# A fused attention and two-MLP kernel: one group's v rows in another queue, and fixed places for some work of TensorE, ScalarE and VectorE

## The chip, the cores and the metric

One core of one Trainium2 chip. The metric is device time in microseconds for one execution, as the median of the runs; lower is better. The engines are TensorE (PE; its weight loads are PEld), VectorE (DVE), ScalarE (ACT), GpSimd (POOL) and SyncE (SP). Each runs its own queue of instructions in order; SP issues most of the DMAs.

## The reference, cut to what matters

```python
# attention: q, k, v are (2, 8, 768, 64), float32
k_sum = k.reshape(B, H, 24, 32, D).max(axis=3)
v_sum = v.reshape(B, H, 24, 32, D).mean(axis=3)
scores_l = where(|i - j| < 16, scale * q @ k.T, -1e9)        # local window
scores_s = scale * q @ k_sum.T + log(32)                     # 24 block summaries
a = softmax(concat([scores_l, scores_s]))                    # over both parts
x = a @ concat([v, v_sum])                                   # 1536 tokens x 512
# first MLP: 512 -> 2048 -> 512
h = maximum(x @ w_in, 0);  y = (h * h) @ w_out
# second MLP: 512 -> 1536 -> 512
xn = y / sqrt(mean(y * y) + 1e-6) * rms_g
out = (silu(xn @ w_gate) * (xn @ w_val)) @ w_out2
```

The MLP weights arrive as float64 and are turned into float32 on the chip.

## The kernel before, in words

Attention runs in 12 groups of 128 tokens, six to a batch. A group g goes through `scores(g)` (TensorE: a mask product, 32 small matmuls, and a second mask product for the first four groups), `softmax(g)` (DVE finds the maximum, ACT takes the exponentials head by head with their sum, DVE divides), `ptrans(g)` (TensorE transposes the probabilities, ACT copies them to pT) and `av(g)` (TensorE multiplies pT by the v rows in `vx`; the output of group 0 is called x0, of group 1 x1). `split_xs` then writes x as a high part (`xhi`, ACT) and a low part (`xlo`, DVE), because every MLP product is made of three float32r products. `qprep(g)` transposes q for groups g and g+1. `vx` has four slots; groups 0 and 1 fill them first.

The weights come in units of 512 KB: `load64` issues the DMA, `conv_a` (two ACT operations, L203 and L204) and `conv_b` (four DVE operations, L210 to L217) turn the words into float32, `split` (one ACT, one DVE operation, L223 and L224) makes the high and low parts. The first eight units are wi0 to wi3 and wo0 to wo3. The table `FIRST` (L227) says behind which other instruction conv_a (key 1) or conv_b (key 2) of a unit must come in its engine's queue.

The program is traced in one order, and a planner lays out each engine's queue from that order and from modelled times; it runs before the kernel is compiled. `after(...)` and `tc.issue_after` bind an instruction to come later than another in the queue of that same engine; they add no wait between engines. Buffers, PSUM banks and DMA landings add real waits.

At the seam between the two MLPs, `turn` transposes the normalised rows and forms their differences (`ta`, `xt`, `bt`). The second MLP multiplies half its columns by a scheme of seven products, for which `late(m)` (L899) makes the high and low parts of the operands T3 and T4 and `latest(m)` (L949) those of B22. `hsplit` (L619) makes the high and low parts (`hhi`, `hlo`) of a hidden tile, which the last `y` matmuls of the first MLP read.

Other names in the rows: `kr`, `qr`, `vr`, `raw_wi`, `raw_wo` are landed inputs, `pps`, `qps`, `xps`, `s`, `h`, `y` are PSUM tiles, `mx` and `sm` the maxima and sums of a softmax, `r` the squared hidden tile, `vsum` a sum of v for batch 1.

Of the kernel before, what the change touches and what calls it, by code (L numbers as in the profile page):

```python
# [10 lines left out]
F32 = mybir.dt.float32  # L11
# [4 lines left out]
ALU = mybir.AluOpType  # L16
# [16 lines left out]
def tile_window_attention_moe_moe2(  # L33
# [13 lines left out]
    nc = tc.nc  # L47
    B, H, S, D = q.shape
    NT, DM = out.shape
    P = 128  # L50
# [5 lines left out]
    NPAIR = H // 2  # L56
    QT = 64
    KW = QT + 2 * WIN
    NK = NB + KW
# [160 lines left out]
    def split(x, nm):  # L220
# [4 lines left out]
        return hi, lo  # L225

    FIRST = {  # L227
        (2, 0): [("mx", 0)], (2, 2): [("xlo", 0, 1)], (2, 3): [("xlo", 1, 1)],
        (1, 1): [("exp", 1)], (1, 2): [("xhi", 0, 1)], (1, 3): [("xhi", 1, 1)],
    }  # L230

    def combine(g, v_, f):
# [98 lines left out]
    def after(*marks):  # L331
        es = ExitStack()
        for m in marks:
            es.enter_context(tc.issue_after(mark[m].ins))
        return es
# [85 lines left out]
    def qload(g):  # L421
        b, r = divmod(g, GPB)
        state[("q", g)] = token_chunk(q, b, r // 2, f"qr{g}")

    def qprep(g):
        qr = state.pop(("q", g))
        qT2 = ap_.tile([P, NPAIR, 2 * P], F32, tag="qT", name=f"qT{g}", bufs=QB)
        for j in range(2):
            ps = psA(f"qps{g}_{j}", [P, NPAIR, P])
            for p in range(NPAIR):  # L430
                nc.tensor.transpose(ps[:, p, :], qr[:, j, p * P : (p + 1) * P], ident)
            with after(*((("exp", 1),) if g == 2 else ())):
                nc.scalar.mul(qT2[:, :, j * P : (j + 1) * P], ps, scale)
        state[("qT", g)] = state[("qT", g + 1)] = qT2

    def vmean(b, c):
# [41 lines left out]
    def scores(g):  # L478
        b, r = divmod(g, GPB)
        qT = state[("qT", g)][:, :, (r % 2) * P : (r % 2 + 1) * P]  # L480
        sl = [psA(f"s{e}_{g}", [P, NPAIR, NK]) for e in range(2)]
        wide = [P, NPAIR, NK]
        if g < NPE:
            for s_ in sl:
                mh = mhi["mid" if r else "first"]
                nc.tensor.matmul(s_, identr, mh.unsqueeze(1).to_broadcast(wide), start=True, stop=False)
        for p in range(NPAIR):
            for x in range(2):
                for e in range(2):
                    u = (e + x) % 2  # L490
                    o = STEP * (2 * r + u)
                    rr = slice(QT * e, QT * e + QT)
                    mark[("s", g)] = nc.tensor.matmul(  # L493
                        sl[e][QT * u : QT * u + QT, p, :],
                        qT[rr, p, QT * u : QT * u + QT],
                        kT[rr, p, o : o + NK],
                        start=g >= NPE, stop=g >= NPE,
                    )
        if g < NPE:
            for s_ in sl:  # L500
                mark[("s", g)] = nc.tensor.matmul(
                    s_, identr, mlo.unsqueeze(1).to_broadcast(wide), start=False, stop=True
                )
        state[("s", g)] = sl
# [66 lines left out]
    def av(g):  # L571
        pT = state.pop(("pT", g))
        ps = psA(f"xps1_{g}")
        for u in range(2):
            for p in range(NPAIR):
                o = p * P + QT * u
                for e in range(2):
                    nc.tensor.matmul(  # L578
                        ps[QT * e : QT * e + QT, o : o + QT],
                        vx[:, (2 * g + u) % NVX, 2 * p + e, :],  # L580
                        pT[:, e * NPAIR + p, QT * u : QT * u + QT],
                        start=True, stop=True,
                    )
        split_xs(ps, g, 1)
        state["done"] = g

# [13 lines left out]
    def hi_lo(hi, lo, s, n):  # L600
        sv = s[:, 0 : n * P].rearrange("d (k s) -> d k s", k=n)
        nc.scalar.copy(hi, sv)
        nc.vector.tensor_tensor(lo, sv, hi.bitcast(F32), op=ALU.subtract)


    def mm3(ps, pairs):
        tot = 3 * len(pairs)
# [10 lines left out]

    def hsplit(s, n, nm):  # L619
        hi, lo = t2(f"hhi{nm}", F32R), t2(f"hlo{nm}", F32R)  # L620
        nc.scalar.copy(hi[:, 0:n], s[:, 0:n])  # L621
        nc.vector.tensor_tensor(lo[:, 0:n], s[:, 0:n], hi[:, 0:n].bitcast(F32), op=ALU.subtract)  # L622
        return hi, lo

    def ff_out(ys, hh, ww, first, last):
# [106 lines left out]
        vm_load(0, c)  # L732
    vload(0)
    qload(2)
    for j in (0, LK - WIN):
        nc.gpsimd.memset(kT[:, :, j : j + WIN], 0.0)
    nc.gpsimd.memset(vx[0:WIN, 0], 0.0)
# [4 lines left out]
    qprep(0)  # L742
    prep_kend(0, nc.vector, 0, 4)
    prep_kend(0, nc.gpsimd, 4, NW1)
    with after("kend"):
        vload(1, nc.gpsimd)
    scores(0)
    softmax(0)
    scores(1)
# [11 lines left out]
    av(0)  # L761
    group(2)
    vload(2)
    rot["tags"] = ("y",)
    group(3)
    rot["tags"] = ("a", "x")
    av(1)
    vload(3)
    ptrans(2)
    qprep(4)  # L770
# [128 lines left out]
    def late(m):  # L899
        if m == 0:  # L900
            new_xs(2, "t")
        hi, lo = (t[:, :, m * P : (m + 1) * P] for t in xs[("t", 2)])
        hi_lo(hi, lo, rows.pop(m), KD)

    for i in range(n1 + 2):
        if i < n1:
            r, c, f = steps1[i]
            if c == 0:
                units1.until(("wi", f))
            if r == len(ROUNDS1) - 1 and c == NCH - 1:  # L910
                units1.cap = NW - 2
            ps = psB.tile([P, CH], F32, tag="h", name=f"h{c}_{f}", bufs=2)
            product(ps, W[("wi", f)], xs[(1, c)], 0, MT)
            t = square(ps, f"{c}_{f}")
            units1.tick()
            hq[i] = hsplit(t, CH, f"{c}_{f}")
        if i >= 2:
            r, c, f = steps1[i - 2]
            first = f == FIRST1[r]
            last = f == FIRST1[r] + ROUNDS1[r] - 1  # L920
            if c == 0:
                units1.until(("wo", f))
            if first:
                for m in range(MT):
                    ys[m] = y_tile(c, m, "y")
            ff_out([ys[m] for m in range(MT)], hq.pop(i - 2), W[("wo", f)], first, last)
            if c == NCH - 1:
                units1.used += 2
            if last:
                for m in range(MT):  # L930
                    gather(MT * c + m, ys.pop(m), r, ROUNDS1, "y", done1)
        if turns:
            turn()
        if i < n1 and norms:
            norm(norms.pop(0))
        if i == n1:
            for m in range(MT):
                late(m)


    hand.close()
# [68 lines left out]
    def pair(r, fill):  # L1010
        fs = (FIRST2[r], FIRST2[r] + 1)
        wg, wv, cs = {}, {}, {}
        for f in fs:
            units1.until(("wv", f))
            for d, kd in ((wg, "wg"), (wv, "wv")):
                d[f] = [
                    [half(t.rearrange("p (k f) -> p k f", k=KD), j) for t in W[(kd, f)]] for j in range(2)
                ]
            cm = W[("cm", f)]
            cs[f] = [[cm[:, e, j].rearrange("p (k f) -> p k f", k=K2) for e in range(2)] for j in range(4)]  # L1020
        A, C, z0, z1, v1 = {}, {}, {}, {}, {}
        for f in fs:
            A[f] = bank("h", f"qa{f}")
            six(A[f], wg[f][0], b1[0], True)
            z0[f] = t2(f"s{f}")
            nc.scalar.copy(z0[f], A[f])
        for f in fs:
            C[f] = bank("a", f"qb{f}")
            six(C[f], wg[f][1], b1[1], True)
            nc.vector.tensor_tensor(z0[f], C[f], z0[f], op=ALU.add)  # L1030
            nc.scalar.activation(z0[f], z0[f], AF.Silu)
        if r == 0:
            for m in (0, 2):
                latest(m)
        units1.tick()
        fill(fs[0])
        for f in fs:
            six(A[f], cs[f][1], x2_, False)
            z1[f] = t2(f"u{f}")
            nc.scalar.copy(z1[f], A[f])  # L1040
        for f in fs:
            C[f] = bank("a", f"qc{f}")
            six(C[f], cs[f][0], x1, True)
        units1.tick()
        for f in fs:
            six(A[f], cs[f][2], x3, False)
            v1[f] = t2(f"v{f}")
            nc.scalar.copy(v1[f], A[f])  # L1048
            nc.vector.tensor_tensor(v1[f], C[f], v1[f], op=ALU.add)  # L1049
        fill(fs[1])  # L1050
        units1.tick()
        for f in fs:
            six(A[f], wv[f][1], x4, False)
            nc.vector.tensor_tensor(z0[f], A[f], z0[f], op=ALU.mult)
            hq[(0, f)] = hsplit(z0[f], CH, f"z0_{f}")
        for f in fs:
            six(C[f], cs[f][3], b22, False)
            nc.vector.tensor_tensor(z1[f], C[f], z1[f], op=ALU.add)
            nc.scalar.activation(z1[f], z1[f], AF.Silu)
            nc.vector.tensor_tensor(z1[f], z1[f], v1[f], op=ALU.mult)  # L1060
            hq[(1, f)] = hsplit(z1[f], CH, f"z1_{f}")
        units1.tick()
# [86 lines left out]
```

## Time and profile before

| | us |
|---|---|
| median of 3 runs (lowest, highest) | 643.59 (642.15, 643.83) |
| the profiled execution | 642.17 |
| its span, first to last instruction | 640.5 |
| TensorE busy in the span | 622.3 (97%) |
| VectorE busy | 457.2 (71%) |
| ScalarE busy | 366.1 (57%) |
| mean granted TensorE clock, share of full | 0.994 |

The profiled execution is the fastest but one of the four known; 1.67 us of its time lie outside the span. Busy TensorE does not mean TensorE at its best: its clock has a lower level, and a matmul counts as busy for twice as long there.

### The profile page before, as it was taken

Reading aid. Unit: us, or ns where it says so; the run is one execution under the profiler, and the core shown is the slowest. Engines: PE = TensorE matmul, PEld = TensorE weight load, DVE = VectorE, ACT = ScalarE, POOL = GpSimd, SP = SyncE. Lnnn points to the kernel's source line nnn. Section 1 sums busy time; section 2 is a strip of 40 time slices with the busy share of each in tenths; the row PEclk is TensorE's granted clock in tenths of the full one; section 3 lists DMA queues with packets and bytes.
Section 4 is the critical chain, followed back from the end, with each engine's and each line's share of the span. In section 5 each row is a group of like instructions: output and inputs, shape, how many; then the busy total and the mean of one; then the engine's idle time right before and its main releaser. Section 6 shows DMA issues by size and latency. Waiting matters only on the chain.

```text
span 640.5 us, 9547 instructions
## 1 busy us (share of the span) xinstructions
PE 622.3 (97%) x3578; PEld 514.2 (80%) x3578; DVE 457.2 (71%) x830; ACT 366.1 (57%) x767; POOL 58.2 (9%) x87
## 2 busy tenths in 40 slices
PE   8879999999999999999999999999999999999997
PEld 6467887888888888888888788888888888888885
DVE  3789767969995299985487779489499499561323
ACT  5677676677673267564554667457357277353241
POOL 5012210000000000000000000003004004012040
PEclk9979999999999999999999999999999999999999
DMA  9999812446232123311020105218528429017063
GB/s 252 294 208 196 160 40 50 120 144 192 71 106 92 34 65 100 99 67 34 0 92 8 34 36 195 67 35 180 116 66 161 103 65 183 15 13 120 1 99 98
DMA packets 84430, 64.19 MB, mean 100 GB/s; under 512 B 50368, under 2 KB 73920, under 8 KB 84384
## 3 DMA queue, kind: packets, MB, share of 16 engines
q1 hardware_dynamic: 72976, 51.32, 27.1%
q0 software_dynamic: 11408, 12.26, 13.5%
q8 instruction: 28, 0.46, 0.3%
q14 instruction: 18, 0.15, 0.1%
HBM read 49.94 MB, written 13.63 MB: 99 GB/s over the span
## 4 chain that ended last, share of the span: by engine, by line
PE 86%; DVE 5%; SPq 4%; DMA 2%; ACT 2%; issue 1%; ACTq 0%
PE h L611 19%; PE y L631 18%; PE z L631 15%; PE qa L965 10%; PE v L611 5%; PE g L611 5%; PE qc L965 5%; PE qb L965 3%; SPq L358 2%; PE xps L578 1%; PE s L493 1%; PE pps L555 1%; SPq L474 1%; DMA raw_wi<-in_moe_w_in_dram 1%; PE xps L595 1%
## 5 line engine op out<-in xcount | busy, mean ns | idle before, releaser
L611 PE MATMUL h<-xhi,w_wi 128*128 128x512 f32 (+1 forms) x480 | 132.1, 349 | 0.0
L631 PE MATMUL y<-w_wo,hhi 128*128 128x512 f32 x384 | 117.0, 393 | 2.1 <-ACT hhi L621 1.6
L611 PEld LDWEIGHTS h<-xhi,w_wi 128*128 128x128 f32 x480 | 84.7, 189 | 12.0 <-ACT t L535 0.2
L631 PE MATMUL z<-w_wp,hhiz 128*128 128x512 f32 x288 | 85.7, 390 | 0.0
L631 PEld LDWEIGHTS y<-w_wo,hhi 128*128 128x128 f32 x384 | 71.3, 188 | 17.7 <-ACT hhi L621 2.3
L611 PE MATMUL h<-xlo,w_wi 128*128 128x512 f32 (+1 forms) x240 | 83.4, 349 | 0.4 <-DVE xlo L569 0.3
L1000 POOL DMA_DIRECT2D out_dram<-zs x40 | 35.0, 1131 | 498.9 <-ACT zs L996 496.5
L631 PE MATMUL y<-w_wo,hlo 128*128 128x512 f32 x192 | 72.4, 392 | 0.0
L631 PEld LDWEIGHTS z<-w_wp,hhiz 128*128 128x128 f32 x288 | 53.9, 188 | 11.1
L631 PE MATMUL z<-w_wp,hloz 128*128 128x512 f32 x144 | 53.0, 389 | 0.0
L790 ACT ACTIVATE r<-h 128x512 f32<-128x512 f32 x48 | 28.7, 597 | 38.7 <-PE h L611 38.7
L611 PEld LDWEIGHTS h<-xlo,w_wi 128*128 128x128 f32 x240 | 45.4, 189 | 6.5 <-DVE xlo L569 1.0
L791 DVE TENSOR_TENSOR r<-h,r 128x512 f32<-128x512 f32 x48 | 32.9, 685 | 21.5 <-ACT r L790 21.3
L631 PEld LDWEIGHTS y<-w_wo,hlo 128*128 128x128 f32 x192 | 35.7, 188 | 7.4 <-issue 0.2
L621 ACT CAST hhi<-r 128x512 fp32r<-128x512 f32 x48 | 29.7, 620 | 18.4 <-DVE r L791 18.1
L622 DVE TENSOR_TENSOR hlo<-r,hhi 128x512 fp32r<-128x512 f32 x48 | 32.8, 684 | 7.4 <-ACT hhi L621 7.1
L611 PE MATMUL g<-x,w_wg 128*128 128x512 f32 x144 | 34.6, 389 | 0.0
L611 PE MATMUL v<-x,w_wv 128*128 128x512 f32 x144 | 34.6, 389 | 0.0
L996 ACT COPY zs<-z 128x512 f32<-128x512 f32 x48 | 26.8, 591 | 11.9 <-PE z L631 11.0
L1049 DVE TENSOR_TENSOR v<-qc,v 128x512 f32<-128x512 f32 x12 | 8.3, 692 | 34.3 <-ACT v L1048 34.3
L631 PEld LDWEIGHTS z<-w_wp,hloz 128*128 128x128 f32 x144 | 27.0, 188 | 5.7
L611 PEld LDWEIGHTS g<-x,w_wg 128*128 128x128 f32 x144 | 27.0, 188 | 5.6
(206 smaller groups left out, 1222.9 us busy)
## 6 DMA issues: line engine op xcount, KB each, us to landing
out_dram<-zs POOLq DMA_DIRECT2D x40, 256.0 KB, 6.4
raw_wi<-in_moe_w_in_dram SPq DMA_DIRECT2D x16, 512.0 KB, 5.2
raw_wo<-in_moe_w_out_dram SPq DMA_DIRECT2D x16, 512.0 KB, 4.8
raw_wg<-in_moe_w_gate_dram SPq DMA_DIRECT2D x12, 512.0 KB, 3.5
raw_wv<-in_moe_w_val_dram SPq DMA_DIRECT2D x12, 512.0 KB, 3.6
raw_wp<-in_moe_w_out_dram SPq DMA_DIRECT2D x12, 512.0 KB, 5.5
kr<-in_k_dram SPq DMA_DIRECT2D x12, 256.0 KB, 4.1
qr<-in_q_dram SPq DMA_DIRECT2D x12, 256.0 KB, 5.1
```

The costliest lines, as they stand in the source:

```text
L358: nc.sync.dma_start(t[:, j].rearrange("p (h d) -> p h d", h=H), src[b, :, o : o + P, :].rearrange("h p d -> p h d"),)
L474: (eng or nc.sync).dma_start(vx[j : j + n, i0 + u], v[b, :, o : o + n, :].rearrange("h s d -> s h d"))
L611: pe["last"] = nc.tensor.matmul(ps, a_, b_, start=(i == 0), stop=(i == tot - 1))
L621: nc.scalar.copy(hi[:, 0:n], s[:, 0:n])
L622: nc.vector.tensor_tensor(lo[:, 0:n], s[:, 0:n], hi[:, 0:n].bitcast(F32), op=ALU.subtract)
L631: pe["last"] = nc.tensor.matmul(y, a_[:, ms], b_, start=(first and i == 0), stop=(last and i == 2))
L790: nc.scalar.activation(t, ps, AF.Relu)
L791: nc.vector.tensor_tensor(t, ps, t, op=ALU.mult)
L965: last = nc.tensor.matmul(ps, w[a_][:, kk], x[b_][:, kk], start=start and n == 0, stop=n == 3 * K2 - 1, skip_group_check=not start,)
L996: nc.scalar.copy(s, ys.pop(m))
L1000: nc.gpsimd.dma_start(out[g * P : (g + 1) * P, :], s, accum_op=ALU.add)
L1049: nc.vector.tensor_tensor(v1[f], C[f], v1[f], op=ALU.add)
```

## The change

The four DMAs of group 1's v rows leave POOL's queue, where they followed the last k summary copy, for SP's queue, where they follow the load of the second weight, wi1; that load is now written right behind `qload(2)`. In TensorE's queue every matmul of av(1) comes behind the scores of group 2, and every small matmul of scores(3) behind av(1); av(1) is written before group 3. Four entries of `FIRST` change: conv_a of wi1 comes behind the q copy for group 2 and the pT copy of group 1, conv_b of wi2 behind the maxima of group 2, conv_a of wi3 behind the exponentials of group 2. The casts and subtractions of `late` and `latest` come behind the last `hsplit` in the queues of ACT and DVE.

```diff
     FIRST = {
-        (2, 0): [("mx", 0)], (2, 2): [("xlo", 0, 1)], (2, 3): [("xlo", 1, 1)],
-        (1, 1): [("exp", 1)], (1, 2): [("xhi", 0, 1)], (1, 3): [("xhi", 1, 1)],
+        (2, 0): [("mx", 0)], (2, 2): [("mx", 2)], (2, 3): [("xlo", 1, 1)],
+        (1, 1): [("qT", 2), ("pT", 1)], (1, 2): [("xhi", 0, 1)], (1, 3): [("exp", 2)],
     }
...
-                nc.scalar.mul(qT2[:, :, j * P : (j + 1) * P], ps, scale)
+                mark[("qT", g)] = nc.scalar.mul(qT2[:, :, j * P : (j + 1) * P], ps, scale)
...
+                    with after(*((("av", 1),) if g == 3 else ())):
+                        mark[("s", g)] = nc.tensor.matmul(   # scores, arguments as before
...
+                    with after(*((("s", 2),) if g == 1 else ())):
+                        mark[("av", g)] = nc.tensor.matmul(  # av, arguments as before
...
+    def behind_h():
+        es = ExitStack()
+        for i in pe["h"]:
+            es.enter_context(tc.issue_after(i.ins))
+        return es
...
     def hsplit(s, n, nm):
         hi, lo = t2(f"hhi{nm}", F32R), t2(f"hlo{nm}", F32R)
-        nc.scalar.copy(hi[:, 0:n], s[:, 0:n])
-        nc.vector.tensor_tensor(lo[:, 0:n], s[:, 0:n], hi[:, 0:n].bitcast(F32), op=ALU.subtract)
+        pe["h"] = (
+            nc.scalar.copy(hi[:, 0:n], s[:, 0:n]),
+            nc.vector.tensor_tensor(lo[:, 0:n], s[:, 0:n], hi[:, 0:n].bitcast(F32), op=ALU.subtract),
+        )
...
     qload(2)
+    units1.load(2)
+    vload(1)
...
-    with after("kend"):
-        vload(1, nc.gpsimd)
...
     group(2)
     vload(2)
+    av(1)
     rot["tags"] = ("y",)
     group(3)
     rot["tags"] = ("a", "x")
-    av(1)
...
             for m in range(MT):
-                late(m)
+                with behind_h():
+                    late(m)
...
             for m in (0, 2):
-                latest(m)
+                with behind_h():
+                    latest(m)
```

## Rows read from the trace of the kernel before

**Rows 1.** The page, granted TensorE clock in tenths, 40 slices of 16 us.

```profile
PEclk9979999999999999999999999999999999999999
```

**Rows 2.** Waits of TensorE: who, for whom, total us, times, longest us.

```profile
PE pps L555 <- DVE t L545: 4.4, 2, 4.2
...
PE y L631 <- ACT hhi L621: 1.6, 2, 1.2
```

**Rows 3.** Windows: length, busy PE, PEld, DVE, ACT, POOL, clock, DMA share, GB/s.

```profile
24.70:64.00 39.30, 31.34 (x373) 25.83 (x373) 32.33 (x64) 29.39 (x86) 7.74 (x6) 0.91 1.08 235
34.00:36.00 2.00, 0.00 (x0) 0.00 (x0) 2.00 (x7) 2.00 (x13) 0.00 (x0) 0.74 1.04 236
36.00:42.00 6.00, 4.81 (x45) 4.06 (x46) 3.99 (x9) 5.22 (x23) 1.44 (x2) 0.52 0.98 156
```

**Rows 4.** Timeline of PE: start, us, instructions, idle before and its releaser.

```profile
26.04 0.57 PE L578 MATMUL xps<-pT,vx 120*64 120x64 f32 x12
29.08 0.70 PE L486 MATMUL s<-mstage 128*128 128x480 f32 x2 [2.48 <-ACT pT L558]
...
32.31 0.70 PE L501 MATMUL s<-mstage 128*128 128x480 f32 x2
37.19 1.08 PE L555 MATMUL pps<-ident,t 128*120 128x128 f32 x4 [4.18 <-DVE t L545]
38.06 1.06 PE L431 MATMUL qps<-ident,qr 128*128 128x128 f32 x4
```

**Rows 5.** Timeline of ACT, early stretch.

```profile
26.84 0.66 ACT L203 ACTIVATE x_wi<-raw_wi 128x512 f32<-128x512 f32 x1 [2.53 <-DMA raw_wi<-in_moe_w_in_dram]
...
33.54 0.36 ACT L535 ACTIVATE t<-s,mx 128x120 f32<-128x120 f32 x1 [1.27 <-DVE mx L529]
```

**Rows 6.** Timeline of DVE, early stretch.

```profile
27.54 0.43 DVE L210 TENSOR_SCALAR x_wi<-x_wi 128x512 f32<-128x512 f32 x1 [2.85 <-ACT x_wi L203]
...
30.67 0.69 DVE L224 TENSOR_TENSOR w_wi<-x_wi,w_wi 128x512 fp32r<-128x512 f32 x1 [0.68 <-ACT w_wi L223]
...
32.79 0.65 DVE L529 TENSOR_REDUCE mx<-s 128x4 f32<-128x480 f32 x1
...
39.69 0.17 DVE L543 TENSOR_SCALAR sm<-sm 128x8 f32<-128x8 f32 x1 [1.20 <-ACT t L535]
...
42.78 0.69 DVE L569 TENSOR_TENSOR xlo<-xps,xhi 128x512 fp32r<-128x512 f32 x1 [1.49 <-ACT xhi L568]
```

**Rows 7.** Timeline of SP's queue: start, time of the issues, DMAs.

```profile
13.19 4.12 SPq L474 DMA_DIRECT2D vx<-in_v_dram  x4
...
20.98 1.91 SPq L188 DMA_DIRECT2D raw_wi<-in_moe_w_in_dram  x3
...
26.88 6.52 SPq L358 DMA_DIRECT2D qr<-in_q_dram  x2
```

**Rows 8.** DMA issues from 13.5, 21.0, 21.9 and 26.9 us: last, us to landing.

```profile
vx<-in_v_dram SPq DMA_DIRECT2D x1, 32.0 KB, 7.7
...
raw_wi<-in_moe_w_in_dram SPq DMA_DIRECT2D x1, 512.0 KB, 5.8
...
raw_wi<-in_moe_w_in_dram SPq DMA_DIRECT2D x1, 512.0 KB, 6.3
...
qr<-in_q_dram SPq DMA_DIRECT2D x1, 256.0 KB, 9.4
```

**Rows 9.** Timeline of PE, ACT and DVE at the seam of the MLPs.

```profile
346.98 1.15 ACT L602 CAST xhit<-xt 128x512 fp32r<-128x512 f32 x2
...
349.85 0.60 ACT L790 ACTIVATE r<-h 128x512 f32<-128x512 f32 x1
...
351.41 0.68 DVE L791 TENSOR_TENSOR r<-h,r 128x512 f32<-128x512 f32 x1
...
354.07 2.11 PE L631 MATMUL y<-w_wo,hhi 128*128 128x512 f32 x8 [1.23 <-ACT hhi L621]
...
362.36 0.39 PE L965 MATMUL qa<-xhi,cm 128*128 128x512 f32 x1
```

More of the change, by code (lines that the diff above doesn't have):

```diff
@@ L492, in scores @@
                     rr = slice(QT * e, QT * e + QT)
[L493 to L498, printed above, removed]
+                    with after(*((("av", 1),) if g == 3 else ())):
+                        mark[("s", g)] = nc.tensor.matmul(
+                            sl[e][QT * u : QT * u + QT, p, :],
+                            qT[rr, p, QT * u : QT * u + QT],
+                            kT[rr, p, o : o + NK],
+                            start=g >= NPE, stop=g >= NPE,
+                        )
         if g < NPE:
@@ L577, in av @@
                 for e in range(2):
[L578 to L583, printed above, removed]
+                    with after(*((("s", 2),) if g == 1 else ())):
+                        mark[("av", g)] = nc.tensor.matmul(
+                            ps[QT * e : QT * e + QT, o : o + QT],
+                            vx[:, (2 * g + u) % NVX, 2 * p + e, :],
+                            pT[:, e * NPAIR + p, QT * u : QT * u + QT],
+                            start=True, stop=True,
+                        )
         split_xs(ps, g, 1)
@@ L620, in hsplit @@
         hi, lo = t2(f"hhi{nm}", F32R), t2(f"hlo{nm}", F32R)
-        nc.scalar.copy(hi[:, 0:n], s[:, 0:n])
-        nc.vector.tensor_tensor(lo[:, 0:n], s[:, 0:n], hi[:, 0:n].bitcast(F32), op=ALU.subtract)
+        pe["h"] = (
+            nc.scalar.copy(hi[:, 0:n], s[:, 0:n]),
+            nc.vector.tensor_tensor(lo[:, 0:n], s[:, 0:n], hi[:, 0:n].bitcast(F32), op=ALU.subtract),
+        )
         return hi, lo
```

## The prediction

> **What bounds the kernel now.** I read the page's slices first. TensorE is busy in nine tenths of almost every slice, and its granted clock is full everywhere but in the third slice [rows 1]. So a gain can come from two sources alone: stretches in which TensorE stands, and the stretch at the lower clock. The waits of TensorE put the largest stall on the softmax of a group and a smaller one on `hhi`, the high part of a hidden tile [rows 2]. The windows then give a size to the early stretch: from 24.7 to 64 us TensorE is busy 31.34 of 39.30 us, so it stands for 7.96 us [rows 3]. From 34 to 36 us it does nothing and the mean clock is 0.74; from 36 to 42 us the clock is 0.52, its lower level (1.2 of 2.4 GHz) for most of that time, and the 4.81 us of work there would take some 2.4 us less at the full one [rows 3].
>
> The timelines say why it stands. After x0 ends at 26.61 TensorE waits 2.48 us for ACT before the scores of group 2 [rows 4]. ACT had nothing wrong with it but its order: conv_a of the second weight, wi1, stood ahead of the q and pT copies and waited 2.53 us for wi1 to land [rows 5]. That is the releaser one step behind the one that the wait names. Then the scores of groups 2 and 3 run until 33.01, and TensorE waits 4.18 us for the first transposes of group 2 at 37.19 [rows 4]. Those wait for the exponentials, which ACT starts at 33.54 behind the maxima [rows 5], which DVE starts at 32.79 [rows 6].
>
> At the other end, at 354.07, the last `y` matmuls wait 1.23 us for `hhi` [rows 9]. ACT casts two pieces of T3 and T4 at 346.98, takes the relu at 349.85, and DVE squares it at 351.41 [rows 9]; the hidden tile stood finished while the operands of the next MLP were made.
>
> **The change part by part.**
>
> *conv_a of wi1 behind the copies; conv_b of wi2 behind the maxima.* These remove nothing, they reorder. The scores of group 2 can follow x0 at 26.6 instead of 29.08: 2.48 us earlier. The distance from their start to the maxima was 32.79 − 29.08 = 3.71 us. The two score groups together take 33.01 − 29.08 = 3.93 us, so one takes 1.97, and without a conv_b in between the maxima can follow at 28.6: 4.2 us earlier. By the same distances the exponentials start 4.2 us earlier, at 29.3, and the transposes of group 2 at 33.0 instead of 37.19.
>
> *x1 between the two scores.* It adds no work. Twelve matmuls of x0 took 0.57 us, so the 32 of x1 take at most 1.5; they stand in the stretch that is empty now. The scores of group 3 move behind them, to about 30.1 to 32.1, and nothing needs those before the exponentials of group 2 are through. The rest of the stall is some 0.9 us, against 4.18, which the first hidden tile can fill, as x1 is split earlier. Before, the clock was still full in the slice with the 2.48 us stall (16 to 32 us) [rows 1] and fell in the longer one [rows 3, 4]; I take it to stay full. What x1 needs, the v rows, is the cost of the next part.
>
> *The v rows on SP.* POOL loses four issues; SP gets them at about 21.9, behind wi1. Four such issues took SP 4.12 us for group 0's rows [rows 7], and the last to land of those that I list took 7.7 us from its issue [rows 8]. So group 1's rows land between 26 us (a short queue: wi1, issued at 20.98, took 5.8 us [rows 7, 8], and the rows follow it) and 34 us (21.9 + 4.12 + 7.7). x1 wants them at 28.6. I take 28.6 to 29.5: the POOL traffic of the same bytes is gone from the time before, so the queue ahead is shorter. The wait is then at most 0.9 us, and behind it on TensorE stand the scores of group 3 only. Behind the rows on SP stand six weights, the first `vsum` and the q of group 4; each is issued up to 4.12 us later. Below nothing too: the same bytes pass the same DMA queues, and leave them less full before 20 us, so these could land as early as now. I take 1.5 us later for all, nearer to the low end because the DMA share is at 1.04 around 34 us [rows 3], that is, the DMA engines rather than SP's issues set the landings there.
>
> The Trainium skill, "DMA: Bandwidth & Descriptors", section "Issuing engines are not separate DMA queues", says that DMAs from any engine end on the same sixteen DMA engines and that the choice of issuer only saves issue time; by that alone the later weights would land as now, and the sum would not change. Its section "Queues, rings and completion order" speaks against the change: descriptors of one queue are taken in order, while different queues are served in turn, so what stood beside the weights now stands ahead of them. The trace shows weights landing in their order of issue, 26.8 and then 28.2 us, worked from [rows 8].
>
> *How much of the 4.2 us lasts.* Behind 43 us DVE is the tight engine: it is busy 32.33 of 39.30 us [rows 3], and 2.85 us of what it stands idle lie ahead of 27.54, where the landing of wi1 holds it as before [rows 6]. The idle time that an earlier softmax can fill is 0.68 + 1.20 + 1.49 = 3.37 us [rows 6]; with some 0.3 us in shorter gaps (an estimate, the rest of the window's idle time being in the pieces that I do not list) it is 3.7. TensorE alone would give back more, but its hidden tiles wait for DVE's conversions. I take 3.7 us for the early stretch. From there to 346 us TensorE hardly waits [rows 2], so the gain is carried to the end.
>
> *conv_a of wi3 behind the exponentials of group 2.* It moves two ACT operations of 0.66 us [rows 5] off a place where x1 would put them now that it is early. Cost nothing, with the exponentials as cover; without that entry 1.3 us would stand ahead of them.
>
> *T3, T4, B22 held.* ACT loses up to four casts ahead of `hhi` and DVE as many subtractions; two casts take 1.15 us [rows 9]. The hidden tile is done at 347, so relu, square and `hhi` can be through at about 350, 3 us before TensorE wants it at 352.84. The 1.23 us stall goes, all of it. What is held must be there by 362.36, where the first product of combined operands starts, or later [rows 9]; held work of 2.4 us on each engine that starts at 350 ends before 358 even with the other seam work between. If that cover failed, ACT's copies of the first products would be late by up to 1.2 us and eat the gain. I take 1.2.
>
> **The sum**: 3.7 + 1.2 = 4.9 us. The profiled execution took 642.17 us (span 640.5 and 1.67 outside), which gives 637.3. It is 1.4 us under the median of the runs, 643.59; on that median the forecast is 638.7 us. A measurement of this kernel tells about 0.3%, 1.9 us, from no change.
>
> **The rivals.**
>
> *The next weight takes the place of the one removed.* conv_a of wi2 comes right behind xhi of x0, so ahead of the exponentials of group 2. If wi2 lands 4.12 us later than its 28.2 [rows 8], at 32.3, conv_a ends at 33.6, just where the exponentials begin now, and the early gain is between nothing and 1 us. With the seam 1.2 to 2.2 us: 642.4 to 641.4. For it speaks that ACT made this very mistake with wi1 [rows 5]; against it, that the queue ahead is lighter by POOL's bytes.
>
> *TensorE is the bound and takes all.* The 7.96 us of standing and the 2.4 us of low clock come back but for about 3 us, and the seam gives 1.2: a gain of 8.6, 635.0. For it speaks that the planner may find other work while DVE converts; against it, that DVE has only 3.7 us to give.
>
> *The q of group 4 comes too late (slower).* Its transposes stand right behind the first ones of group 2, at 38.06 [rows 4], and TensorE's order lets nothing pass. q landed at 36.3 [rows 8]. If its issue slips by S, TensorE stands until 36.3 + S. The old time is lost from S = 1.8, and the seam's gain too from S = 3.0. The bound of S is 4.12 us of issues, or near 5.5 if v rows meet the queue that q met, whose two issues took 6.52 us [rows 7]. At S = 5.5 it is 5.5 − 3.0 = 2.5 us slower: 646.1. Against it: the planner lays out the order with later loads in view, and can put the transposes behind the first hidden tile.
>
> *The order does not take hold.* If rows or slots keep x1 where it was, only the seam counts: 642.4. ACT's wait for wi1 is then still gone, so this is not likely.
>
> **How the numbers follow.** The forecast 0.50, with its own range 637 to 641; TensorE takes all 0.17; the next weight 0.19; the slower case 0.08; no hold 0.06. Faster by over 0.3% are the first two, and half of the third: 0.75. Within 0.3%: the rest of the third, the last, and a little of the slower case, 0.18. Slower: 0.07. The range leaves out the far ends of the two outer cases: 634.8 to 643.0.
>
> **What would show it.** Right: scores of group 2 within 1 us behind x0; the maxima at 28 to 30 us; the first `pps` of group 2 at 33 to 34.5 us; no clock below full behind 30 us; DVE without a gap over 0.7 us from 28 to 58; the `y` matmuls of the seam with no wait for `hhi`. Wrong: an ACT wait for `raw_wi` ahead of the exponentials; a TensorE wait for `vx` or `qr` over 2 us; copies of `qa` late at the start of the second MLP; or a planner's new order that opens stalls between 64 and 346 us, where there are none now, which the rows of before can't show.

## The result, and the profile after

The median after is 647.32 us (646.12 to 648.52, 5 runs) against 643.59 us before (5 runs); the ratio is 1.0068, 95% interval 1.0049 to 1.0087. The change makes the kernel slower, by 3.7 us between the two medians and by 4.4 us at that ratio, where 4.9 us of gain were forecast (638.7 us, with a range of 634.8 to 643.0). The profiled execution has a span of 645.6 us.

Both stretches that the prediction worked on came out near its figures in size, though not by its path. The page's clock line of after, for [rows 1], shows 9 in the third slice, where 7 stood, and an 8 each in the fourth and the ninth (129 to 145 us). So the sign "no clock below full behind 30 us" failed: the granted clock was full from 30 to 56 us and 0.50 from 58 to 60 us, behind waits of 1.17 and 0.78 us for `xhi` and `r`.

```profile
PEclk9998999989999999999999999999999999999999
```

The waits of TensorE in after, for [rows 2] (who, for whom, total us, times, longest):

```profile
PE h L619 <- ACT xhi L569: 3.5, 3, 1.6
PE h L619 <- DVE xlo L570: 2.6, 4, 1.1
PE pps L556 <- DVE t L546: 2.2, 3, 1.7
PE y L641 <- ACT hhi L630: 1.5, 1, 1.5
```

The 4.2 us wait for a softmax is gone, and many shorter ones, for x, for softmaxes and for a hidden tile, are new. The same windows as [rows 3]:

```profile
24.70:64.00 39.30, 33.33 (x399) 27.86 (x398) 35.16 (x68) 30.38 (x89) 8.06 (x6) 0.96 1.07 236
34.00:36.00 2.00, 1.83 (x16) 1.63 (x14) 2.00 (x7) 2.00 (x6) 0.00 (x0) 1.00 1.17 265
36.00:42.00 6.00, 3.95 (x37) 3.01 (x37) 6.00 (x14) 6.00 (x23) 1.80 (x1) 1.00 0.88 146
```

TensorE does 26 more matmuls in 24.7 to 64 us (399 against 373), and DVE is busy 2.83 us more. The timeline of TensorE, for [rows 4]:

```profile
26.36 0.70 PE L486 MATMUL s<-mstage 128*128 128x480 f32 x2
...
28.61 1.15 PE L580 MATMUL xps<-pT,vx 120*64 120x64 f32 x32
29.69 1.05 PE L494 MATMUL s<-kT,qT 64*64 64x120 f32 x32
...
36.68 0.62 PE L556 MATMUL pps<-ident,t 128*120 128x128 f32 x4 [0.85 <-DVE sm L545]
```

The scores of group 2 start at 26.36 instead of 29.08, x1 has its v rows in time, and the stall of 4.18 us ahead of the first `pps` of group 2 has shrunk to 0.85. At the seam, for [rows 9], `hhi` now comes ahead of the held cast on ACT, and the window 340 to 370 us, which holds the last `y` matmuls in both kernels, has no gap on TensorE (30.00 us busy; before, 28.77):

```profile
357.70 0.62 ACT L630 CAST hhi<-r 128x512 fp32r<-128x512 f32 x1 [0.85 <-DVE r L801]
358.23 1.66 ACT L604 CAST xhit<-xt 128x512 fp32r<-128x512 f32 x3
```

The rows of before show one thing more. What stood directly ahead of `hhi` there was the cast of a weight, w_wv, which had itself waited for a `y` matmul; the square was ready at 351.41 + 0.68 = 352.09 us [rows 9]:

```profile
352.88 0.62 ACT L223 CAST w_wv<-x_wv 128x512 fp32r<-128x512 f32 x1 [1.93 <-PE y L631]
353.41 0.61 ACT L621 CAST hhi<-r 128x512 fp32r<-128x512 f32 x1
```

In after this cast comes at 360.31 us, behind the held ones. The edit does not bind it; the planner moved it.

So the loss lies between. SP's first load for the second MLP is a landmark: from it to the end of the span every run below takes the same time but for the seam. Here it is before, and then after (start, time of the issue):

```profile
230.48 0.38 SPq L188 DMA_DIRECT2D raw_wg<-in_moe_w_gate_dram  x1
```

```profile
237.41 0.38 SPq L188 DMA_DIRECT2D raw_wg<-in_moe_w_gate_dram  x1
```

After is 6.93 us late there, and takes 408.2 us from there to the end against 410.0 before, 1.8 us less: the seam's gain. Where the 6.93 us arise is seen in the order of TensorE around group 6, the first of batch 1. Before (timeline of TensorE; left out between 86.66 and 92.80 are the other matmuls of the 48 for `h`):

```profile
82.19 1.05 PE L493 MATMUL s<-kT,qT 64*64 64x120 f32 x32
83.17 1.15 PE L578 MATMUL xps<-pT,vx 120*64 120x64 f32 x30
84.25 1.04 PE L413 MATMUL vmean<-vsum,indv 96*24 96x512 f32 x2
85.22 1.51 PE L493 MATMUL s<-kT,qT 64*64 64x120 f32 x32
86.66 0.50 PE L611 MATMUL h<-xhi,w_wi 128*128 128x256 f32 x2
...
92.80 1.03 PE L555 MATMUL pps<-ident,t 128*120 128x128 f32 x8
```

And after (left out: the rest of the 48, `vmean`, `y` matmuls between and behind the halves of the scores of group 7, and what follows 98.78):

```profile
78.94 1.15 PE L580 MATMUL xps<-pT,vx 120*64 120x64 f32 x30
80.76 0.50 PE L619 MATMUL h<-xhi,w_wi 128*128 128x256 f32 x2 [0.68 <-ACT xhi L569]
...
87.18 1.05 PE L494 MATMUL s<-kT,qT 64*64 64x120 f32 x32
...
89.13 1.04 PE L494 MATMUL s<-kT,qT 64*64 64x120 f32 x16
...
93.29 1.04 PE L494 MATMUL s<-kT,qT 64*64 64x120 f32 x16
...
98.78 1.06 PE L556 MATMUL pps<-ident,t 128*120 128x128 f32 x8 [1.69 <-DVE t L546]
...
109.43 0.51 PE L619 MATMUL h<-xhi,w_wi 128*128 128x256 f32 x2 [1.61 <-ACT xhi L569]
110.97 0.39 PE L619 MATMUL h<-xlo,w_wi 128*128 128x256 f32 x1 [1.04 <-DVE xlo L570]
```

The last matmuls of x5 (the 30 at 83.17 and at 78.94) end 4.23 us earlier than before. Then the 48 matmuls of the third pass's hidden tiles (I call them h_2) run ahead of the scores of group 6. Before, they stood behind the scores of group 7 and filled the 6 us in which the softmax of group 6 was made. Now that softmax starts 5 us later than before, in spite of the lead, and TensorE has less to do while it runs. Two windows balance the account, each from the end of x5 to SP's first `raw_wo` issue behind 140 us, which frees at the same piece of work in both (before, then after):

```profile
84.32:146.38 62.06, 60.68 (x649) 51.99 (x650) 48.53 (x83) 46.48 (x136) 2.02 (x2) 1.00 0.31 88
```

```profile
80.09:153.32 73.23, 65.59 (x681) 55.31 (x682) 50.76 (x84) 46.38 (x136) 2.48 (x2) 0.95 0.26 75
```

The 32 matmuls more in after are the scores of group 6, 1.05 us, which before were done by 83.24; for equal work the lead was 4.23 − 1.05 = 3.2 us. The stretch took 11.17 us longer: 1.05 for these; 6.26 because TensorE stands 7.64 us instead of 1.38; and the mean clock of 0.95 over 73 us makes up to 3.7 more, 11.0 in all. So 3.2 us of lead became 6.9 us of lag.

### The profile page after: what moved, and what is told of

The parts are those of the page before. It is cut to its first block, busy times and chain, and to the rows that moved or that the text cites. A ratio compares the mean times of both kernels' runs of the same rounds, so it can differ in the third digit from the quotient of the medians.

```text
span 645.6 us, 9554 instructions
## 1 busy us (share of the span) xinstructions
PE 625.7 (97%) x3578; PEld 516.9 (80%) x3578; DVE 457.3 (71%) x830; ACT 365.1 (57%) x767; POOL 56.6 (9%) x83
## 4 chain that ended last, share of the span: by engine, by line
PE 88%; DVE 5%; ACT 3%; DMA 2%; SPq 1%; issue 1%; DVEq 0%; ACTq 0%
PE h L619 20%; PE y L641 19%; PE z L641 15%; PE qa L976 10%; PE v L619 5%; PE g L619 5%; PE qc L976 5%; PE qb L976 3%; PE xps L580 1%; DMA kr<-in_k_dram 1%; PE s L494 1%; PE pps L556 1%; ACT t L536 1%; PE xps L597 1%; DVE t L522 1%
## 5 line engine op out<-in xcount | busy, mean ns | idle before, releaser
L619 PE MATMUL h<-xhi,w_wi 128*128 128x512 f32 (+1 forms) x480 | 135.4, 355 | 4.7 <-ACT xhi L569 3.5
L641 PE MATMUL y<-w_wo,hhi 128*128 128x512 f32 x384 | 118.7, 396 | 2.0 <-ACT hhi L630 1.5
L619 PEld LDWEIGHTS h<-xhi,w_wi 128*128 128x128 f32 x480 | 86.8, 194 | 18.0 <-ACT xhi L569 4.8
L619 PE MATMUL h<-xlo,w_wi 128*128 128x512 f32 (+1 forms) x240 | 84.9, 355 | 2.6 <-DVE xlo L570 2.6
L641 PEld LDWEIGHTS z<-w_wp,hhiz 128*128 128x128 f32 x288 | 53.9, 188 | 11.1
L619 PEld LDWEIGHTS h<-xlo,w_wi 128*128 128x128 f32 x240 | 46.7, 194 | 9.2 <-DVE xlo L570 3.7
L1007 ACT COPY zs<-z 128x512 f32<-128x512 f32 x48 | 26.8, 593 | 11.9 <-PE z L641 11.0
```

The costliest lines, as they stand in the source:

```text
L619: pe["last"] = nc.tensor.matmul(ps, a_, b_, start=(i == 0), stop=(i == tot - 1))
L641: pe["last"] = nc.tensor.matmul(y, a_[:, ms], b_, start=(first and i == 0), stop=(last and i == 2))
L1007: nc.scalar.copy(s, ys.pop(m))
```

## The experiments

Three theories stood at the start. A: the new order around group 6 costs the time. B: the moved loads cost it (weights, v sums and q stand behind the v rows on SP), and the order only shows it. C: the seam's holding costs somewhere else. All ratios are against the kernel before on the same chip. With each edit the planner lays out all queues anew, so a run can differ from its neighbour in more than its diff; the orders named below are read from the traces.

**The seam alone.** Before, with only the casts and subtractions of `late` and `latest` behind the last `hsplit`:

```diff
             for m in range(MT):
-                late(m)
+                with behind_h():
+                    late(m)
... (the same for latest; behind_h and hsplit as in the change)
```

> The kernel before with one part of the change: T3, T4 and B22 held behind the last hidden tile's split in the queues of ACT and DVE. The early stretch is as before. Both theories below: the 1.23 us wait for hhi at the seam goes and nothing takes its place, 1.2 us faster than before, ratio 0.998. Rival of this part: the held casts make the first copies of the second MLP late and the time is the same.

Measured: 641.13 us, ratio 0.9969 (0.9952 to 0.9987). The `hhi` wait at the seam is gone. C falls. From the landmark to the end it takes 408.4 us.

**The loads alone.** Before, with only the loads moved:

```diff
     qload(2)
+    units1.load(2)
+    vload(1)
...
-    with after("kend"):
-        vload(1, nc.gpsimd)
```

> The kernel before with one part of the change: wi1 behind the q of group 2 and the v rows of group 1 behind it, both on SP. In the laid-out order of TensorE 36 of the 48 matmuls of the third pass's hidden tiles (h_2) now stand ahead of the scores of group 6. Theory A (order: this places the stock of MLP work ahead of the scores of batch 1, so nothing covers their softmax): slower than before by 2 to 6 us, ratio 1.003 to 1.009, with TensorE waits for the softmax between 95 and 130 us. Theory B (data: the k rows and the v sum of batch 1 land later, the order only follows): also slower, but with TensorE or POOL waiting for landings. Theory C (the early reorder costs): no slower than before.

Measured: 650.54 us, ratio 1.0118 (1.0092 to 1.0145), the landmark 8.0 us late. h_2 stands ahead of the scores of group 6 here too (36 of the 48 from 82.05, the scores at 87.05). The loss is larger than A's 1.009, and the waits for the softmax that A named between 95 and 130 us are not there; TensorE's largest waits are for `hhi` and `xhi`, as in after:

```profile
PE y L631 <- ACT hhi L621: 4.3, 3, 2.7
PE h L611 <- ACT xhi L568: 3.8, 4, 1.6
```

So the loads bring the order with them, and this run can't part A from B.

**Everything but the loads.**

```diff
-    units1.load(2)
-    vload(1)
...
+    with after("kend"):
+        vload(1, nc.gpsimd)
```

> The change without the move of the loads: the v rows of group 1 stay on POOL; the four FIRST entries, the order x0, scores 2, x1, scores 3 and the seam part are in. Its laid-out order has the scores of groups 6 and 7 ahead of all of h_2, as the kernel before. x1 still waits for late v rows in the model of the planner, so the first transposes of group 2 stand ahead of x1. Theory A: no loss behind 80 us, the seam's 1.2 us and up to 2 us of the early stretch: 1 to 3 us faster than before, ratio 0.995 to 0.998. Theory C: slower than before by 2 us or more.

Measured: 644.43 us, ratio 1.0022 (1.0008 to 1.0037). Neither A's gain nor C's loss of 2 us or more came. h_2 stands behind the scores of group 7, but another wait had opened on TensorE:

```profile
35.10 1.08 PE L556 MATMUL pps<-ident,t 128*120 128x128 f32 x4 [6.21 <-DVE sm L544]
```

Without the early v rows the planner puts x1, and with it the scores of group 3, behind these transposes. Right behind them TensorE waits 2.13 us more, for the q of group 4 to land.

**The changed kernel with h_2 held.** Here and below, "the hold" is this edit in `h_pair`:

```diff
+            with after(*((("s", GPB + 1),) if k_ == 2 else ())):
                 product(ps[:, G2 * j : G2 * (j + 1)], W[("wi", f + j)], ...)
```

> The changed kernel with one addition: in TensorE's queue all matmuls of h_2 come behind the scores of group 7. Loads, early order and seam are as in the changed kernel. Theory A: the scores of group 6 run at about 80 us behind x5 without a wait (their summary copy on POOL ended at 77.8 us in the changed kernel), the waits between 98 and 130 us shrink below 2 us in all, and the early 4.2 us and the seam's 1.2 us are kept: 638 us, ratio 0.990 to 0.994 to the kernel before. Theory B: TensorE stands at the scores of group 6 or at the v sum product until about 87 us, and the time stays at 645 to 648 us, ratio 1.003 to 1.008.

Measured: 639.93 us, ratio 0.9956 (0.9935 to 0.9976): 1.1% less than the changed kernel, some 7 us, by one place in one queue. A's range (0.990 to 0.994) is just missed; as A said, the waits between 98 and 130 us shrink below 2 us. The data of batch 1 is now what group 6 waits for:

```profile
PE vmean L413 <- DMA vsum<-in_v_dram: 2.0, 1, 2.0
PE s L494 <- POOL kT L398: 1.5, 1, 1.5
```

That much is right of B. (This profile is of an execution of 642.15 us, 2.2 above the kernel's median.)

**The order alone, in the kernel before.** All loads, the table and the seam as before; h_2 traced ahead of group 6, and no longer in the third pass (those lines are left out):

```diff
...
         if g == GPB - 1:
-            group(GPB)
+            h_pair(2, 0)
+            h_pair(2, 2)
+            with inline():
+                scores(GPB)
+            vload(GPB)
+            softmax(GPB)
+            qload(GPB + 2)
```

> The kernel before, with one thing changed: the 48 matmuls of the third pass's hidden tiles stand ahead of the scores of group 6 on TensorE, as in the changed kernel; loads, the table and the seam are those of before. Theory A (the order alone costs): 5 to 8 us over the kernel before, ratio 1.008 to 1.012, with waits for hhi, xhi and the softmax of groups 6 and 7 between 90 and 140 us, and a clock below full there. Theory B (the order costs only together with loads that come late for an attention that is 4 us ahead): within 2 us of before, ratio 0.997 to 1.003, and no such waits.

Measured: 657.66 us, ratio 1.0228 (1.0207 to 1.0249), the landmark 16.7 us late. A is confirmed with more than its size; in this version the third pass's `y` matmuls stand in one piece too, and its timeline of TensorE shows the waits of after in a larger size, the longest for the pT of a later group:

```profile
91.20 1.05 PE L493 MATMUL s<-kT,qT 64*64 64x120 f32 x32
...
102.43 1.29 PE L555 MATMUL pps<-ident,t 128*120 128x128 f32 x8 [2.08 <-DVE t L545]
...
138.39 1.86 PE L578 MATMUL xps<-pT,vx 120*64 120x64 f32 x29 [5.86 <-ACT pT L558]
```

An order with h_2 ahead costs without late data, then. B's "within 2 us" is off by 13. As more of the order changed than the place of h_2, the 2.28% is not the price of that place alone.

**The hold and an earlier v sum.** The changed kernel, the hold, and:

```diff
-    units1.load(8)
     nc.sync.dma_start(vsum, v[1]...)
+    units1.load(8)
```

> The changed kernel with those 48 matmuls held behind the scores of group 7, as in the run before, and with the first DMA of the v sums issued ahead of the ninth weight instead of behind it. If the 1.5 us that the scores of group 6 waited for the k summary and the 2.0 us that the v-sum product waited for its DMAs are what is left of the early gain, both waits shrink by over half, the clock in 80 to 100 us rises above 0.95, and the time falls another 2 to 4 us below the run with the hold alone: 636 to 638 us, ratio 0.988 to 0.992. If the DMA engines rather than the place of issue set when the sums land, it stays at 0.995 to 0.997.

Measured: 639.48 us, ratio 0.9953 (0.9937 to 0.9970). Both waits are gone, and the clock is 1.00 from 80 to 146 us, but the time is that of the hold alone. It is the number of the second branch without its cause: the sums no longer come late. The window of this run that answers to those above (end of x5 to the `raw_wo` issue), and its three longest waits from 80 to 146 us:

```profile
80.24:145.53 65.29, 61.74 (x681) 52.23 (x682) 50.45 (x84) 46.16 (x136) 2.02 (x2) 1.00 0.29 84
```

```profile
PE pps L556 <- DVE t L546: 1.1, 1, 1.1
PE y L641 <- ACT hhi L630: 0.8, 1, 0.8
PE y L641 <- DVE hlo L631: 0.5, 1, 0.5
```

For equal work x5 is 84.32 − 80.24 − 1.05 = 3.03 us ahead of before; TensorE then stands 3.55 us instead of 1.38, 2.17 more; and the `raw_wo` issue and the landmark are 0.85 and 0.86 us ahead, which is 3.03 − 2.17.

In its early stretch this run shows a wait that the changed kernel's profile does not have, for the q of group 4:

```profile
39.93 1.09 PE L431 MATMUL qps<-ident,qr 128*128 128x128 f32 x4 [2.41 <-DMA qr<-in_q_dram]
```

With the hold alone this wait is 0.99 us. The lead of 3.03 us is what is left behind it.

**The earlier v sum without the hold.** The changed kernel with that edit alone:

```diff
-    units1.load(8)
     nc.sync.dma_start(vsum, v[1]...)
+    units1.load(8)
```

> The changed kernel with the first DMA of the v sums issued ahead of the ninth weight, and no hold: 46 of the 48 matmuls of the hidden tiles still stand ahead of the scores of group 6. Theory A (the order costs): 644 to 648 us, ratio 1.003 to 1.009, waits for hhi, xhi and the softmax behind 98 us as in the changed kernel. Theory B (late sums cost): under 641 us, ratio under 0.996.

Measured: 647.33 us, ratio 1.0069 (1.0050 to 1.0089), as the changed kernel; 46 of the 48 still stand ahead, and the waits are for `hhi` and `xhi` again (none for the softmax of group 6). Late sums are not the cause, and not by themselves what makes the planner choose that order.

**The table and the seam.** Before, with the four entries of `FIRST` and the seam's edit; loads and x1 as before.

```diff
-        (2, 0): [("mx", 0)], (2, 2): [("xlo", 0, 1)], (2, 3): [("xlo", 1, 1)],
-        (1, 1): [("exp", 1)], (1, 2): [("xhi", 0, 1)], (1, 3): [("xhi", 1, 1)],
+        (2, 0): [("mx", 0)], (2, 2): [("mx", 2)], (2, 3): [("xlo", 1, 1)],
+        (1, 1): [("qT", 2), ("pT", 1)], (1, 2): [("xhi", 0, 1)], (1, 3): [("exp", 2)],
```

> The kernel before with the four entries of the table changed and T3, T4 and B22 held; group 1's v rows stay on POOL and x1 and the scores of group 3 keep their places; the hidden tiles of the third pass stay behind the scores of group 7. If the loss without the moved loads came from x1 standing ahead of the scores of group 3, this has no 6 us wait for the softmax of group 1, ACT's wait for the second weight is gone, and 2 to 3 us of the early stretch stay besides 1.2 to 2 us of the seam: about 639 us, ratio 0.991 to 0.995. If the table alone brings nothing without the v rows: the seam alone, 0.996 to 0.998.

Measured: 641.15 us, ratio 0.9978 (0.9963 to 0.9992): no more than the seam alone. ACT's copies are early, but with x1 in its old place TensorE only waits longer in one piece:

```profile
36.77 1.08 PE L555 MATMUL pps<-ident,t 128*120 128x128 f32 x4 [6.51 <-DVE t L545]
```

**The loads and the hold.** Before, with the moved loads and the hold:

```diff
+    units1.load(2)
+    vload(1)
...
-    with after("kend"):
-        vload(1, nc.gpsimd)
...
+            with after(*((("s", GPB + 1),) if k_ == 2 else ())):
                 product(ps[:, G2 * j : G2 * (j + 1)], W[("wi", f + j)], ...)
```

> The kernel before with only the loads moved (as in the second run, which was 1.2% slower), and the 48 matmuls of the third pass's hidden tiles held behind the scores of group 7. If the loss of that run was the order too: at least two thirds of it comes back, ratio 0.997 to 1.004. If v rows on SP cost by themselves (the weights, v sums and q behind them): it stays above 1.007.

Measured: 643.43 us, ratio 1.0008 (0.9996 to 1.0020). Of 1.18% loss 1.10% comes back: the loads themselves cost at most 0.2%, and nothing that is clear of noise.

**The hold and the early v sum, without the rule for x1.**

```diff
-                    with after(*((("av", 1),) if g == 3 else ())):   # scores
...
-                    with after(*((("s", 2),) if g == 1 else ())):    # av
...
     vload(2)
-    av(1)
     rot["tags"] = ("y",)
     group(3)
     rot["tags"] = ("a", "x")
+    av(1)
```

> The changed kernel with the hold and the early v sum, without the rule that puts x1 between the scores of groups 2 and 3 (x1 behind both, as before). If the rule earns something of its own, by filling the wait for the softmax of group 2: 1 to 2 us slower than the run with the hold and the early v sum, ratio 0.997 to 1.000. If the earlier copies of q and pT are all that the early stretch gives: the same, 0.993 to 0.997.

Measured: 642.79 us, ratio 1.0004 (0.9991 to 1.0017), 0.5% slower than with the rule, a little more than expected. The rule earns some 3 us, provided that the v rows come early; without them (the third run against the eighth) it costs 0.4%. TensorE now stands in two long waits in front of 41 us:

```profile
36.64 1.06 PE L555 MATMUL pps<-ident,t 128*120 128x128 f32 x4 [4.46 <-ACT x_wo L203]
40.44 1.09 PE L431 MATMUL qps<-ident,qr 128*128 128x128 f32 x4 [2.74 <-ACT w_wi L223]
```

The releasers in these rows are inferred, and neither transpose reads a converted weight. The first reads the probabilities of group 2, which DVE finished at 36.49 us; the second reads the q of group 4, which was issued at 29.20 us and took 11.1 us to land, to 40.3. With the rule the same two instructions come no earlier than 36.90 and 39.93 us, but x1, the scores of group 3 and the first hidden tile run in front of them.

**All 48 ahead of the transposes of group 6.** The changed kernel with the early v sum; the two hidden pairs of the third pass are traced behind the second pass's `y` pairs (and no longer in the third) and bound behind the scores of group 7, the transposes of group 6 behind them:

```diff
...
             y_pair(k_, 2)
+        if k_ == 1:
+            h_pair(2, 0)
+            h_pair(2, 2)
+            with inline():
+                ptrans(g + 1)
...
```

> The changed kernel with the early v sum, and the two hidden pairs of the third pass traced behind the fourth y pair and ahead of the transposes of group 6, and bound behind the scores of group 7; so TensorE's order from 80 to 140 us is close to that of before, with all 48 matmuls ahead of the transposes of group 6 instead of 39. If the rest of the early gain was lost to the waits in that order (1.14 us for the softmax of group 6, 0.80 and 0.50 for the hidden tile): the waits go and the time is 2 to 3 us under the run with hold and early v sum, 636 to 638 us, ratio 0.988 to 0.992. If the gain is taken by DVE and ACT, which are no less busy, the waits come back elsewhere: 0.994 to 0.997.

Measured: 643.89 us, ratio 1.0022 (1.0005 to 1.0039). Neither range was met. The wait for the softmax is gone as meant, but the planner now puts half of the scores of group 8 ahead of the `y` matmuls, and these wait for a hidden tile:

```profile
90.50 1.03 PE L556 MATMUL pps<-ident,t 128*120 128x128 f32 x8
91.46 1.04 PE L494 MATMUL s<-kT,qT 64*64 64x120 f32 x16
95.03 2.07 PE L641 MATMUL y<-w_wo,hhi 128*128 128x512 f32 x4 [2.53 <-ACT hhi L630]
```

The clock goes to 0.50 with it, for 8 us (windows of 4 us, columns as in [rows 3]):

```profile
92.00:96.00 4.00, 1.47 (x12) 1.10 (x9) 3.12 (x6) 2.21 (x6) 0.00 (x0) 0.88 0.00 0
96.00:100.00 4.00, 4.00 (x24) 2.44 (x22) 2.30 (x4) 1.07 (x2) 0.00 (x0) 0.50 0.00 0
100.00:104.00 4.00, 4.00 (x38) 3.65 (x38) 1.86 (x3) 1.52 (x5) 0.00 (x0) 0.50 0.28 63
```

**The same without the rule for x1.** The edit of the tenth run on top of that of the eleventh:

```diff
-                    with after(*((("av", 1),) if g == 3 else ())):   # scores
-                    with after(*((("s", 2),) if g == 1 else ())):    # av
```

> As the run before it, without the rule that puts x1 between the scores of groups 2 and 3. The two differ in that rule alone, in front of 40 us; if the rule is worth 1 to 2 us, this one is slower by that, and if it is worth nothing, the same within 0.2%.

Measured: 646.25 us, ratio 1.0053 (1.0033 to 1.0072), 0.3% slower, some 2 us: the rule's worth once more, though here the two intervals overlap.

All together, with the landmark against that of before and the stretch from it to the end of the span:

| kernel | ratio | h_2 ahead of scores 6 | landmark, us | to the end, us |
|---|---|---|---|---|
| before | 1 | no | 0 | 410.0 |
| after | 1.0068 | yes | +6.9 | 408.2 |
| seam alone | 0.9969 | no | −0.9 | 408.4 |
| loads alone | 1.0118 | yes | +8.0 | 409.7 |
| all but the loads | 1.0022 | no | +4.3 | 408.5 |
| after, hold | 0.9956 | no | +1.8 | 408.2 |
| before, order forced | 1.0228 | yes | +16.7 | 409.9 |
| after, hold, early v sum | 0.9953 | no | −0.9 | 408.2 |
| after, early v sum | 1.0069 | yes | +7.0 | 408.2 |
| table and seam | 0.9978 | no | +0.3 | 408.4 |
| loads, hold | 1.0008 | no | +0.8 | 409.7 |
| as the eighth line, no rule for x1 | 1.0004 | no | +2.7 | 408.2 |
| all 48 ahead of the transposes | 1.0022 | no | +4.3 | 408.2 |
| the same, no rule for x1 | 1.0053 | no | +6.1 | 408.2 |

The last column has two values, 409.7 to 410.0 without the seam's edit and 408.2 to 408.5 with it. With h_2 ahead the kernel loses some 7 us in each of three pairs that differ by the hold: after, the loads alone, and after with the early v sum. The seam alone has a landmark 0.9 us early although nothing ahead of it was edited, so differences of a microsecond in that column are within what executions differ by. Most of that 0.9 is there before anything edited runs: x0 ends at 25.83 us in the seam alone, at 26.61 in before. Counted from the end of x0, the seam alone is 0.1 us early at the landmark, and the version with the hold and the early v sum (x0 ends at 26.66) 0.9.

## Why the prediction was wrong

The step that failed is this: "From there to 346 us TensorE hardly waits, so the gain is carried to the end." It took the absence of waits in [rows 2] for slack that would let a lead through, while that absence belonged to the order that the planner had laid out with the old loads. With the moved loads it laid out another, 50 us behind the edit, and this order cost 7 us: 3.2 us of lead at the end of x5 became 6.9 us of lag at the landmark, and in three pairs of runs binding h_2 back to its place gave the 7 us back.

- *The early stretch, 3.7 us.* Right in size: 3.2 us of lead for equal work at the end of x5. Its path was another. The maxima came at 30.0, not 28.6, and the first `pps` of group 2 at 36.68, not 33.0. "Without a conv_b in between" was wrong: conv_b of wi1 still stood ahead of the maxima on DVE (27.15 to 30.09 us). Nor did "by the same distances" hold: the way from the first exponentials (31.13 us) to the `pps` grew from 3.65 to 5.55 us, with conversions of weights between the steps of the softmax on ACT and DVE. What kept TensorE going was x1, the scores of group 3 and 24 matmuls of the first hidden tile in front of it. The prediction had this filling as the smaller part.
- *x1 between the scores.* Costed at no work and no gain of its own; it is worth 2 to 3 us with the early rows, and costs without them.
- *The v rows on SP.* Four issues took 2.43 us on SP at 20.33, not 4.12, and x1 did not wait. The last row issued landed at about 26 us, the low end of the stated range (whose working had the rows behind wi1 and yet at 26, when wi1 itself was to land at 26.8). With the order held the loads cost 0.1%, not clear of noise. Of the two rules of the Trainium skill, "DMA: Bandwidth & Descriptors", the one in "Issuing engines are not separate DMA queues" agrees with that number, and with the landing of wi2 at 28.2 us in after as in before. Whether the other rule, in "Queues, rings and completion order", ever made a load late no run here shows.
- *The seam, 1.2 us.* Right in size, a little low: 1.5 to 1.8 us. The reason was only half right. The operands' subtractions did delay the square on DVE, but with the square ready at 352.09 us `hhi` could still have met TensorE at 352.84; the cast of w_wv ahead of it made it late. The planner moved that cast as well, which the prediction did not foresee: luck, as far as the sum goes.
- *The carry.* Even in the right order at most about 1 us of the 3 arrives: 0.9 by the landmark, and 0.16% between the ratios 0.9953 and 0.9969, whose intervals overlap. 2.17 us of new waits take the rest, for softmaxes and hidden tiles.
- *The rivals.* None of the four was it in the changed kernel. One of them, the late q of group 4, came in part in other versions: TensorE waited for it 0.99 us with the hold, 2.41 us with the hold and the early v sum, and 2.13 us without the moved loads. That takes part of the early gain, and what an earlier issue of q would give back was not run. The planner's new order stood among the things that would make the forecast wrong, with its place, but without a price or a chance; it should have been the rival on the slow side.

What stays open: why the planner prefers that order once the loads move. It shows in all versions with the loads moved and no hold that were run, and in none with the loads in their old place and nothing forced; the first DMA of the v sums is not enough to undo it. Open too is whether more than 1 us of the early gain can be kept: the attempt to fill the wait for group 6's softmax turned into a wait for the next tile.

The version with the hold and the early v sum, at 0.9953, beats both kernels; against the seam's edit alone its advantage is not shown.

## What to carry to other kernels

Where a planner lays out the queues, an edit's price includes the new order everywhere behind it: compare the order of the engine that bounds the kernel, piece by piece, before counting a local gain as carried. A stretch without waits is no store of slack; work that stands behind a softmax's inputs fills the time that the softmax takes, and the same work in front of them is done just as fast and leaves a hole later. When an edit that looks right comes out slow, bind the one group that moved back to its place: a single `after` showed here that the loss came from that place, and that the moved loads themselves cost next to nothing.

## What the runs showed of the hardware that was not expected

Which stands the clock followed. In the run with all 48 ahead, the wait of 2.53 us was followed by 8 us at the lower level (0.50, 1.2 GHz). In after, TensorE was busy 1.53 us of 108 to 112, with waits of 1.61 and 1.04 us and little work around them, and the next 4 us were granted 0.57:

```profile
108.00:112.00 4.00, 1.53 (x10) 1.32 (x11) 4.00 (x8) 1.38 (x7) 0.00 (x0) 1.00 0.43 98
112.00:116.00 4.00, 4.00 (x23) 4.00 (x22) 3.83 (x6) 3.92 (x7) 0.00 (x0) 0.57 0.00 0
```

From 36 to 42 us of after, with waits of 0.85, 0.15, 0.50, 0.54 and 0.17 us, the clock stayed at 1.00, where before, behind 4.18 us in one piece, it was 0.52 [rows 3, 4]. That is not a property of the edit. In the same stretch of the version with the hold, waits of 0.86 and 0.99 us were followed by 0.50 from 38 to 40 us, and in that with the hold and the early v sum the wait of 2.41 us by 0.50 from 40 to 42 us. So a stall that is broken into shorter ones can still be followed by the lower clock. What decides it no run here separates; the granted clock has to be read from the windows of each run.
